# Pooling the keys and values of all later batches on GpSimd instead of VectorE

## Chip, cores and metric

One of the eight cores of a Trainium2 chip runs the whole kernel. The metric is device time in microseconds (us) from launch to end, lower is better. The kernel before was run three times; the profile is of one more execution.

## What is computed

Attention with pooled keys and values over 8 batches of 8 heads, 576 tokens and 64 channels, then a dense feed-forward layer with a piecewise activation, then a layer of eight experts of which each token takes one. The change touches only the pooling of `k` and `v`: the mean over groups of 8 neighbouring tokens, which leaves 72 pooled rows per head.

```python
B, H, S, D = q.shape                      # 8, 8, 576, 64
k_p = k.reshape(B, H, S // 8, 8, D).mean(axis=3)
v_p = v.reshape(B, H, S // 8, 8, D).mean(axis=3)
scores = (1 / sqrt(D)) * q @ k_p^T
x = softmax(scores) @ v_p                 # 4608 tokens x 512
h = x @ w_in; g = activation(h); x = g @ w_out
...                                       # then each token's expert, from the arg max of x @ w_gate
```

## The kernel before

The 4608 tokens are 36 tiles of 128. They go through the dense layer in ten blocks of two to four tiles. A block has 16 steps (`m`), each a group of matmuls with `w_in` (`f1`, lines 624 to 626) and one with `w_out` (`f2`, lines 665 to 669). Every number is split in two parts for precision, so each product takes three matmuls. The order on each engine is the order in which the program text issues the instructions; nothing reorders them.

Between the matmul groups stand *slots*, two per step. A slot runs the next one or two *units* of the attention of the tiles ahead: transposing `q` (`u_qt`, line 346 for tiles from 9 on), scores (`u_sc`, lines 365 to 385, or `u_sc_all`, lines 305 to 316), the softmax's sum and reciprocal (`finish`, lines 394 to 397) and its product, on VectorE for tiles 9 to 33 (line 399) and on GpSimd for the others (line 407), turning the probabilities (`u_turn_p` and `u_place_p`, by way of the DRAM tensor `p_d`, lines 416 and 422), and the product with the pooled values (`u_pv`, line 442 on TensorE, lines 448 and 449 for its eviction). A slot also runs steps of the routing of the block before (`route_steps`); the last of these are scatters by GpSimd into `perm_d` (line 760), which wait for VectorE's line 746 or 747 and for one another.

Pooling: `load_kv` (line 240) is a DMA on the sync engine's queue (SP) that brings one head's keys or values as 72 rows of 8 x 64 numbers into one of three buffers `RAW`. `pool_kv` adds the eight parts. On VectorE it is one `tensor_reduce` (line 246). On GpSimd it is three additions, of 256, 128 and 64 columns, each of the two halves of what is left (lines 249 to 251). Keys go to `KP` (in tile `AT`), which TensorE transposes (`u_kt`, line 290); values go to `VS`, which line 442 reads. Then the same step issues the load of the head three further on into the buffer just freed, so this load waits for the pooling. Batch 0's and batch 1's keys are pooled in other ways (`head_pool`, `pair_step`); the eight values of batch 1 and all sixteen heads of batches 2 to 7 go through `kv_step`. Of these, batches 2 to 7 (96 heads) use VectorE and batch 1 uses GpSimd.

SP is one queue in order. Besides these loads it holds the loads of `q` for the turned tiles (`load_chunk`, line 227, four DMAs of one 32-row part each), the stores of the split `w_out` (line 612, after VectorE's line 261), and lines 416 and 422. A DMA that waits for an engine holds up all that stand behind it. GpSimd (POOL in the profile) is one queue too: scatters, the products of line 407, the low parts of `w_in` (line 261 called with GpSimd, tile `W`) and, now, the poolings.

Of the kernel before, what the change touches and what calls it, by code (L numbers as in the profile page):

```python
# [23 lines left out]
def attention_ffn_routed_experts_kernel(  # L24
# [12 lines left out]
    nc = tc.nc  # L37
# [67 lines left out]
    def at(o, n, p=128):  # L105
        return AT[0:p, o:o + n]
# [10 lines left out]
    RAW = [at(3264 + 512 * i, 512, SP_) for i in range(3)]  # L117
# [120 lines left out]
    def load_kv(b, i, dst):  # L238
        src = k if i < H else v
        nc.sync.dma_start(out=dst, in_=src[b, i % H].rearrange("(p r) d -> p (r d)", r=8))  # L240

    def pool_kv(b, i, raw, eng):
        h = i % H
        dst = (KP if i < H else VS[:, b % 2])[:, h * D:(h + 1) * D]
        if eng is nc.vector:
            eng.tensor_reduce(out=dst, in_=raw.rearrange("p (r d) -> p d r", r=8), axis=AX.X,
                              op=ALU.add)
            return
        eng.tensor_tensor(out=raw[:, 0:256], in0=raw[:, 0:256], in1=raw[:, 256:512], op=ALU.add)
        eng.tensor_tensor(out=raw[:, 0:128], in0=raw[:, 0:128], in1=raw[:, 128:256], op=ALU.add)  # L250
        eng.tensor_tensor(out=dst, in0=raw[:, 0:D], in1=raw[:, D:2 * D], op=ALU.add)
# [209 lines left out]
    def kv_step(b, i):  # L461
        def f():
            n = (b - 1) * 2 * H + i
            pool_kv(b, i, RAW[n % 3], nc.vector if b > 1 else nc.gpsimd)
            if n + 3 < (B - 1) * 2 * H:
                load_kv(1 + (n + 3) // (2 * H), (n + 3) % (2 * H), RAW[n % 3])
        return f
# [111 lines left out]
    n = FIRST  # L579
# [558 lines left out]
    with tc.manual_schedule():  # L1138
# [124 lines left out]
        for g, (j, m) in enumerate(steps):  # L1263
            if m == 0:
# [11 lines left out]
                if j == 1:  # L1276

                    n = 4 * TURN0 // CHUNK
# [204 lines left out]
```

## Time and profile before

| | |
|---|---|
| three runs | 1439.2, 1444.04 and 1445.14 us, median 1444.04 us |
| the profiled execution's own time | 1442.14 us |
| its span, first to last instruction | 1440.4 us |
| TensorE (PE) busy | 1377.1 us, 96% |
| VectorE (DVE) busy | 862.5 us, 60% |
| ScalarE (ACT) busy | 418.3 us, 29% |
| GpSimd (POOL) busy | 183.5 us, 13% |
| mean granted TensorE clock | 0.984 |

The engines run side by side, so no column adds up to the span. Matmuls overlap each other, and a busy PE can hide a slower step; where PE stands still, the list of its waits says on what. "SPq" is the sync engine's queue, "issue" a time for which the profile names no reason.

### The profile page before, as it was taken

What the parts mean: (1) busy time and instruction counts of PE and PEld (TensorE: products, weight loads), DVE (VectorE), ACT (ScalarE), POOL (GpSimd) and SP (SyncE); (2) the same over time, 40 slices, a digit from 0 to 9 for tenths busy, and PEclk for the clock granted to TensorE, in tenths of its full rate; (3) what the DMA queues carried; (4) which work ended last, traced back from release to release, by engine and by line L of the source; (5) the groups of instructions that cost most, each with busy time, mean ns of one, the idle gap of its engine ahead of it and who ended that gap; (6) DMA issues with size and microseconds to landing.
All of it is one profiled execution on the core that took longest, in us unless ns stands there. A gap on an engine that the chain in (4) does not pass through costs nothing. (4 is left out here: it accounts for less than half of the span.)

```text
span 1440.4 us, 21554 instructions
## 1 busy us (share of the span) xinstructions
PE 1377.1 (96%) x7920; PEld 1114.1 (77%) x7920; DVE 862.5 (60%) x1692; ACT 418.3 (29%) x745; POOL 183.5 (13%) x206
## 2 busy tenths in 40 slices
PE   6799999999999999999999999998999999999996
PEld 5666677777877878788788788887878888888785
DVE  4688869768777866986866555454432323332435
ACT  5344323322222322222222233342111111111334
POOL 3152100001001001000010011012221211110211
PEclk9899999999999999999999999999999999999999
DMA  8565556546546445554553345561533223332514
GB/s 236 160 209 176 161 148 201 188 140 181 148 143 179 150 132 166 163 178 126 169 167 108 110 137 164 189 231 55 188 125 107 90 79 99 108 98 82 175 38 146
DMA packets 170827, 210.69 MB, mean 146 GB/s; under 512 B 84199, under 2 KB 114055, under 8 KB 170696
## 3 DMA queue, kind: packets, MB, share of 16 engines
q1 hardware_dynamic: 136120, 103.74, 24.5%
q10 hardware_dynamic: 26784, 83.96, 18.1%
q0 software_dynamic: 7792, 21.35, 4.7%
q8 instruction: 69, 1.13, 0.3%
q14 instruction: 62, 0.51, 0.1%
HBM read 182.93 MB, written 49.66 MB: 161 GB/s over the span
## 5 line engine op out<-in xcount | busy, mean ns | idle before, releaser
L624 PE MATMUL ps<-XT,W 128*128 128x512 f32 (+2 forms) x640 | 246.0, 384 | 4.8 <-DVE FG L653 3.6
L625 PE MATMUL ps<-XT,W 128*128 128x512 f32 (+2 forms) x640 | 237.7, 371 | 1.8 <-DVE XT L449 1.8
L626 PE MATMUL ps<-XT,W 128*128 128x512 f32 (+2 forms) x640 | 237.4, 371 | 1.0 <-POOL W L261 1.0
L632 ACT ACTIVATE FX<-FX,half 128x512 f32<-128x512 f32 (+2 forms) x152 | 104.0, 684 | 397.9 <-DVE FX L631 356.9
L667 PE MATMUL ps<-WO,FG 128*128 128x512 f32 x528 | 211.4, 400 | 0.4 <-DMA WO<-wo_d 0.4
L668 PE MATMUL ps<-WO,FG 128*128 128x512 f32 x528 | 207.1, 392 | 0.0
L669 PE MATMUL ps<-WO,FG 128*128 128x512 f32 x528 | 206.4, 391 | 0.0
L1029 DVE SCALAR_TENSOR_TENSOR FG<-ps,FG 128x512 fp32r<-128x512 f32 (+1 forms) x64 | 43.2, 675 | 181.7 <-ACT FG L1028 171.8
L624 PEld LDWEIGHTS ps<-XT,W 128*128 128x128 f32 x640 | 121.3, 190 | 31.5 <-DVE FG L653 6.0
L631 DVE TENSOR_SCALAR FX<-ps 128x512 f32<-128x512 f32 (+2 forms) x152 | 96.1, 632 | 81.7 <-PE ps L626 81.7
L625 PEld LDWEIGHTS ps<-XT,W 128*128 128x128 f32 x640 | 121.4, 190 | 21.0 <-DVE XT L449 2.9
L626 PEld LDWEIGHTS ps<-XT,W 128*128 128x128 f32 x640 | 121.3, 190 | 20.1 <-POOL W L261 2.0
L642 DVE TENSOR_TENSOR ps<-FX,ps 128x512 f32<-128x512 f32 (+2 forms) x144 | 92.9, 645 | 58.7 <-ACT FX L632 57.7
L760 POOL DMA_INDIRECT perm_d<-idt,POSI x36 | 35.1, 974 | 710.2 <-DVE SM L746 564.4
L643 ACT ACTIVATE FG<-ps 128x512 fp32r<-128x512 f32 (+2 forms) x144 | 81.1, 563 | 141.4 <-DVE ps L642 134.8
L667 PEld LDWEIGHTS ps<-WO,FG 128*128 128x128 f32 x528 | 99.7, 189 | 23.2 <-issue 2.4
L669 PEld LDWEIGHTS ps<-WO,FG 128*128 128x128 f32 x528 | 99.5, 189 | 21.5
L668 PEld LDWEIGHTS ps<-WO,FG 128*128 128x128 f32 x528 | 99.7, 189 | 18.3
L653 DVE TENSOR_TENSOR FG<-ps,FG 128x512 fp32r<-128x512 f32 (+2 forms) x144 | 91.8, 638 | 35.2 <-ACT FG L643 33.7
L1028 ACT ACTIVATE FG<-ps 128x512 fp32r<-128x512 f32 (+1 forms) x64 | 37.4, 585 | 248.8 <-PE ps L1025 225.5
L1023 PE MATMUL ps<-XT,W 128*128 128x512 f32 (+1 forms) x256 | 98.7, 386 | 2.9 <-ACT XT L1007 2.9
L1024 PE MATMUL ps<-XT,W 128*128 128x512 f32 (+1 forms) x256 | 99.0, 387 | 0.3 <-DVE XT L1008 0.2
(239 smaller groups left out, 2177.5 us busy)
## 6 DMA issues: line engine op xcount, KB each, us to landing
WO<-wo_d ACTq DMA_DIRECT2D x128, 512.0 KB
AT<-in_moe_w_dram SPq DMA_DIRECT2D x10, 2048.0 KB
AT<-in_moe_w_dram SPq DMA_DIRECT2D x14, 1024.0 KB
p_d<-AT SPq DMA_DIRECT2D x25, 384.0 KB
AT<-in_v_dram SPq DMA_DIRECT2D x60, 144.0 KB
wo_d<-WO SPq DMA_DIRECT2D x16, 512.0 KB
AT<-in_k_dram SPq DMA_DIRECT2D x56, 144.0 KB
yrow_d<-Y ACTq DMA_DIRECT2D x7, 1032.0 KB
```

The source lines that it names most:

```text
L624: nc.tensor.matmul(o, wi(m, 0, c), xh, start=(c == 0), stop=False)
L625: nc.tensor.matmul(o, wi(m, 0, c), xl, start=False, stop=False)
L626: nc.tensor.matmul(o, wi(m, 1, c), xh, start=False, stop=(c == KD - 1))
L631: nc.vector.tensor_scalar(r, o, -1.0, 1.0, op0=ALU.max, op1=ALU.min)
L632: nc.scalar.activation(out=r, in_=r, func=ACTF.Square, scale=0.5, bias=half)
L642: nc.vector.tensor_tensor(out=o, in0=r, in1=o, op=ALU.max)
L653: nc.vector.tensor_tensor(out=gl, in0=o, in1=r32(gh), op=ALU.subtract)
L667: nc.tensor.matmul(o, gh, WO[:, g % 4, 0], start=(m == 0), stop=False)
L668: nc.tensor.matmul(o, gh, WO[:, g % 4, 1], start=False, stop=False)
L669: nc.tensor.matmul(o, gl, WO[:, g % 4, 0], start=False, stop=(m == KF - 1))
L1023: nc.tensor.matmul(o, e1(0)[:, c, ms], xh, start=(c == 0), stop=False)
L1024: nc.tensor.matmul(o, e1(0)[:, c, ms], xl, start=False, stop=False)
```

## The change

In `kv_step` the engine is now GpSimd for every batch. Nothing else in the program text is different.

```diff
@@ kv_step @@
             n = (b - 1) * 2 * H + i
-            pool_kv(b, i, RAW[n % 3], nc.vector if b > 1 else nc.gpsimd)
+            pool_kv(b, i, RAW[n % 3], nc.gpsimd)
             if n + 3 < (B - 1) * 2 * H:
                 load_kv(1 + (n + 3) // (2 * H), (n + 3) % (2 * H), RAW[n % 3])
```

96 instructions leave VectorE and 288 come to GpSimd; the orders of PE, ACT and SP stay as they were. Three places matter for what follows.

VectorE before, in the second block, around the first transpose of `q` for a turned tile, line 346 (`VS` is the pooled values, `WG<-Y` belongs to the routing, `FX<-ps`, `ps<-FX` and `FG<-ps` to the activation, `WO<-FX` to the split of `w_out`, `XT<-ps` to the eviction of line 449):

```order
L246 TENSOR_REDUCE VS<-AT 72x64
L653 TENSOR_TENSOR FG<-ps_74,FG 128x512
L261 TENSOR_TENSOR WO<-FX,WO 128x512
L631 TENSOR_SCALAR FX<-ps_73 128x512
L346 STREAM_TRANSPOSE AT<-AT 128x512
L246 TENSOR_REDUCE VS<-AT 72x64
L642 TENSOR_TENSOR ps_73<-FX,ps_73 128x512
L690 STREAM_TRANSPOSE WG<-Y 128x512
L449 SCALAR_TENSOR_TENSOR XT<-ps_79,XT 128x4x128
```

The same piece now:

```order
L653 TENSOR_TENSOR FG<-ps_74,FG 128x512
L261 TENSOR_TENSOR WO<-FX,WO 128x512
L631 TENSOR_SCALAR FX<-ps_73 128x512
L346 STREAM_TRANSPOSE AT<-AT 128x512
L642 TENSOR_TENSOR ps_73<-FX,ps_73 128x512
L690 STREAM_TRANSPOSE WG<-Y 128x512
L449 SCALAR_TENSOR_TENSOR XT<-ps_79,XT 128x4x128
```

The poolings are gone, and with them the one that stood between the transpose of `q` and the activation's line 642.

GpSimd before, from the second block on (all scatters of six blocks follow one another):

```order
L1208 MEMSET WG 128x512
L1209 MEMSET WG 128x128
L1215 COPY WG<-ident 32x4x8 x4
L407 TENSOR_TENSOR AT<-AT,ssm_127 128x576
L760 DMA perm_d<-idt,POSI 36864x1 x24
L407 TENSOR_TENSOR AT<-AT,ssm_127 128x576
```

GpSimd now, in the fourth block, where the keys of batch 4 meet the scatters:

```order
L760 DMA perm_d<-idt,POSI 36864x1
L249 TENSOR_TENSOR AT<-AT 72x256
L250 TENSOR_TENSOR AT<-AT 72x128
L251 TENSOR_TENSOR AT<-AT 72x64
L249 TENSOR_TENSOR AT<-AT 72x256
L250 TENSOR_TENSOR AT<-AT 72x128
L251 TENSOR_TENSOR AT<-AT 72x64
L760 DMA perm_d<-idt,POSI 36864x1
L249 TENSOR_TENSOR AT<-AT 72x256
L250 TENSOR_TENSOR AT<-AT 72x128
L251 TENSOR_TENSOR AT<-AT 72x64
L760 DMA perm_d<-idt,POSI 36864x1
```

Poolings now stand behind scatters and in front of them; this is so in three stretches (batches 3, 4 and 5), while the scatters of the later blocks fall between batches.

SP, the same before and now, in the second block: each load of a head (line 240) waits for a pooling, and the loads of `q` stand behind it:

```order
L240 DMA AT<-in_v_dram 72x512
L227 DMA AT<-in_q_dram 32x9x32 x4
L612 DMA wo_d<-WO 128x1024
L240 DMA AT<-in_v_dram 72x512
L227 DMA AT<-in_q_dram 32x9x32 x4
L240 DMA AT<-in_v_dram 72x512
L227 DMA AT<-in_q_dram 32x9x32 x4
L612 DMA wo_d<-WO 128x1024
```

What moved here is only whom the loads of line 240 wait for: GpSimd's line 251 in place of VectorE's line 246.

## Rows read from the trace of the kernel before

**Rows 1.** The page, busy time, share of the span and instructions of each engine.

```profile
PE 1377.1 (96%) x7920; PEld 1114.1 (77%) x7920; DVE 862.5 (60%) x1692; ACT 418.3 (29%) x745; POOL 183.5 (13%) x206
```

**Rows 2.** Busy time by stretch: length, then PE, PEld, DVE, ACT, POOL; clock, DMA share, GB/s.

```profile
137.00:157.00 20.00, 18.09 (x81) 11.51 (x80) 17.81 (x30) 6.58 (x12) 5.52 (x16) 1.00 0.33 110
...
200.00:260.00 60.00, 55.87 (x365) 43.76 (x364) 54.30 (x104) 19.44 (x34) 3.12 (x3) 1.00 0.61 182
...
460.00:720.00 260.00, 259.56 (x1665) 207.97 (x1664) 199.40 (x366) 73.39 (x120) 7.77 (x8) 1.00 0.52 156
```

**Rows 3.** What PE waited for, 137 to 720 us: total us, times, longest.

```profile
PE ps L698 <- issue: 3.5, 1, 3.5
PE ps L442 <- DMA PT<-p_d: 3.4, 4, 1.7
PE ps L624 <- DVE FG L653: 2.3, 3, 1.2
PE ps L624 <- ACT XT L448: 0.9, 1, 0.9
PE ps L442 <- ACT PT L431: 0.6, 1, 0.6
```

**Rows 4.** Key poolings, batches 2 to 7, on DVE (line 246): ns min/median/max, first and last start.

```profile
L246 DVE TENSOR_REDUCE AT<-AT x48: 1000/1058/1083, 137.7 to 690.7; 72x64 f32<-72x512 f32 x48
```

**Rows 5.** Batch 1's value poolings on POOL, 76 to 106 us: busy, mean ns, idle before.

```profile
L249 POOL TENSOR_TENSOR AT<-AT 72x256 f32<-72x256 f32 x8 | 5.9, 732 | 7.9 <-DMA AT<-in_v_dram 7.9
...
L250 POOL TENSOR_TENSOR AT<-AT 72x128 f32<-72x128 f32 x8 | 3.6, 455 | 0.6
L251 POOL TENSOR_TENSOR VS<-AT 72x64 f32<-72x64 f32 x8 | 2.6, 320 | 0.6
```

**Rows 6.** Timeline of DVE, 179 to 190 us: start, duration, instruction, idle before.

```profile
183.56 0.71 DVE L346 STREAM_TRANSPOSE AT<-AT 128x512 f32<-128x512 f32 x1 [4.17 <-DMA AT<-in_q_dram]
184.20 0.99 DVE L246 TENSOR_REDUCE VS<-AT 72x64 f32<-72x512 f32 x1
185.12 0.68 DVE L642 TENSOR_TENSOR ps<-FX,ps 128x512 f32<-128x512 f32 x1
...
187.46 0.69 DVE L449 SCALAR_TENSOR_TENSOR XT<-ps,XT 128x512 fp32r<-128x512 f32 x1 [1.06 <-ACT XT L448]
```

**Rows 7.** Timeline of PE, 182 to 189.5 us.

```profile
188.26 1.51 PE L698 MATMUL ps<-WG 128*32 128x96 f32 x32 [3.48 <-issue]
```

**Rows 8.** Busy time by stretch, the one with the lower clock; columns as in Rows 2.

```profile
186.70:193.50 6.80, 5.24 (x41) 4.23 (x42) 5.25 (x8) 2.83 (x7) 0.00 (x0) 0.50 0.63 151
```

**Rows 9.** Timeline of SP's queue, 174 to 189 us.

```profile
177.76 0.37 SPq L240 DMA_DIRECT2D AT<-in_v_dram  x1
180.05 1.81 SPq L227 DMA_DIRECT2D AT<-in_q_dram  x4
```

**Rows 10.** What SP's queue waited for, 157 to 184 us.

```profile
SPq L240 <- DVE AT L246: 2.0, 3, 0.8
SPq L227 <- DMA FX<-w_d: 1.9, 1, 1.9
SPq L240 <- DVE VS L246: 0.8, 1, 0.8
```

**Rows 11.** What SP's queue waited for, 137 to 720 us.

```profile
SPq L240 <- DVE AT L246: 148.5, 40, 22.1
```

**Rows 12.** Timeline of POOL, 338 to 358 us (scatters of the third block).

```profile
348.50 0.96 POOL L760 DMA_INDIRECT perm_d<-idt,POSI  x1 [5.29 <-DMA perm_d<-idt,POSI]
```

**Rows 13.** Timelines of POOL and of DVE, 60 to 63.5 us.

```profile
60.42 1.30 POOL L261 TENSOR_TENSOR W<-FX,W 128x512 fp32r<-128x512 f32 x1 [20.46 <-ACT W L572]
...
61.12 0.63 DVE L396 TENSOR_SCALAR ssm<-ssm 128x8 f32<-128x8 f32 x1
```

**Rows 14.** Lines 396 and 399, whole span: ns min/median/max, first and last start.

```profile
L396 DVE TENSOR_SCALAR ssm<-ssm x36: 165/172/628, 23.4 to 873.5; 128x8 f32<-128x8 f32 x36
...
L399 DVE TENSOR_TENSOR AT<-AT,ssm x25: 757/757/760, 207.5 to 805.0; 128x576 f32<-128x576 f32 x25
```

## Prediction
> **What bounds the kernel now.** I read the busy times first. TensorE (PE) is busy for 96% of the span, VectorE (DVE) for 60% [rows 1], but a mean says little, so next comes the table by stretch, from the first pooling that moves (137.7 us) to the last (about 717 us). From 460 to 720 us PE is busy for 259.56 of 260 us: whatever DVE does there, PE sets the pace. In two earlier stretches DVE is the fuller engine: 17.81 of 20 us at 137 to 157 us, 54.30 of 60 us at 200 to 260 us, and there PE has holes [rows 2]. What the change can win is therefore the time for which PE stands still between 137 and 720 us, and the list of PE's waits gives it, item by item [rows 3]. DVE's total isn't the measure.
>
> The largest item is the 3.48 us before line 698, at 188.26 us, for which the list has no name [rows 7]. DVE's timeline explains it. At 183.56 us DVE begins the transpose of `q` of line 346 after 4.17 us of waiting for the load of `q`. Everything behind it is late: a pooling of 0.99 us, line 642, ScalarE's evictions, and line 449, which ends at 188.15 us [rows 6]. Line 449 reads the PSUM bank that line 698 needs next, and PE starts 0.11 us later. The standstill has an aftermath: the granted clock is 0.50 from 186.7 to 193.5 us, the lower of the two levels (1.2 in place of 2.4 GHz), and PE is busy for 5.24 us of that [rows 8]. At full clock the same matmuls would have taken half, so 2.6 us go there.
>
> **The change part by part.** *What leaves DVE*: 96 reductions, 48 of keys at 1.058 us and 48 of values at nearly the same [rows 4], about 101 us in all. None of it counts by itself where PE is full; it counts in the waits below.
>
> *What POOL gets*: 96 times three additions of 732, 455 and 320 ns, 1.51 us a head [rows 5], 145 us in 580 us. POOL is at 13% of the span [rows 1], so it has the time. Costed at nothing, under the cover of the load distance: a head's load is issued three poolings ahead, and its pooled rows are used many slots later. If that cover went, SP would stand, and the second rival prices that.
>
> *The end of the first block (137 to 157 us)*: five reductions (5.3 us) leave a DVE that has 2.2 us of slack there [rows 2]. PE's waits on ScalarE in this stretch, 0.9 us on line 448 and 0.6 us on line 431 [rows 3], come from evictions that run late behind DVE. I take both: **1.5 us**. Bounds: 0, if ScalarE is late by itself; 1.9 us, all of PE's idle time there (20 less 18.09) [rows 2].
>
> *The late load of `q`*: the load's last four DMAs are issued at 180.05 to 181.86 us, behind the head load of 177.76 us [rows 9], and DVE starts at 183.56 us. For PE not to stand, line 449 would have to end 3.48 us sooner. One microsecond of it comes for nothing, since the pooling of 0.99 us between the transpose and line 642 [rows 6] is gone. The load must bring the other 2.5 us. On SP, up to there, 2.0 and 0.8 us were waits for poolings on DVE, and 1.9 us, just before these four, a wait for a load `FX<-w_d` [rows 10], which ScalarE issues behind DVE's work. The first two waits go if POOL is in time, which makes 2.8 us at once; the third shrinks, because five reductions (another 5.3 us) no longer stand in DVE's line ahead of it. So the load moves forward by 2.8 to 4.7 us, a little more than the 2.5 us needed. I take the whole standstill, 3.5 us, and with it the 2.6 us of low clock that followed it: **6.1 us**. Bounds: 0, if the `q` rows are limited by their own transfer; 6.1 us.
>
> *Turned probabilities and the second block*: PE waits 3.4 us, in four places, for `PT<-p_d`, and 2.3 us for DVE's line 653 [rows 3]. The second is DVE's lateness, and goes. The first is a load of line 422 that stood in SP behind head loads, and these waited for DVE in total 148.5 us on keys alone [rows 11]. That sum is mostly waiting that cost nothing, but in these four places the transfer behind it was late. POOL, which stands idle most of the time, answers sooner. **5.7 us**; bounds 0 and 5.7 us.
>
> *What the additions do to DVE*: this is the price that could come back. At 60.42 us POOL runs an addition of 1.30 us until 61.72 us; DVE's line 396, of 8 columns, starts at 61.12 us and takes 0.63 us, until 61.75 us [rows 13], where 0.172 us is its median [rows 14]. It ended with POOL's addition. So a small DVE instruction can lose up to 0.45 us to POOL. The Trainium skill, "SBUF — State Buffer", section "Who interferes with whom", has the rule: DVE and GpSimd share a pair of ports, a `tensor_scalar` can take it, a DVE instruction with two SBUF inputs contends too, and the loser waits for the whole instruction. The trace agrees for line 396; no row shows it for line 399, the two-input product of the turned tiles. By that rule each turned tile would have two exposed instructions, and the sum would be the smaller one that follows here.
>
> The price by rows: POOL pools for 145 of 580 us, so an addition is under way a quarter of the time. Line 396 may lose 0 to 0.45 us. Line 399 [rows 14] shows no loss, so 0 is one end; the other is one longest addition, 0.73 us [rows 5]. For a tile that makes a quarter of 1.2 us, 0.3 us, in a chain which reaches PE only where the probabilities are late. If every one of the four late places lost a full 0.3 us, that would be **1.2 us** given back, and I take that; bounds 0 and 4 times 1.2, 4.7 us.
>
> *Sum*: 1.5 + 6.1 + 5.7 − 1.2 = 12.1 us. The profiled execution's own time is 1442.1 us (its span 1440.4 us, and 1.7 us around it); it becomes 1430.0 us. The median of the three runs is 1.9 us above that execution, so the forecast of a median is **1432 us**. After 720 us the program has the same orders and PE is the pace again, so what is won before stays won.
>
> **The rivals.** *The load of `q` is late anyway.* Its four DMAs of many short rows may be bound by their own transfer and by the load `FX<-w_d` [rows 10], not by poolings. Against: 1.0 us is won in the chain regardless, and most of the SP waits named there are for poolings. For: the margin is small, 2.8 against 2.5 us. Then most of the 6.1 us stays, 12.1 − 6.1 = 6 us are won, and the time is 1438 us, within half a per cent.
>
> *The poolings get stuck behind scatters (slower).* POOL is one queue, and in three stretches poolings stand behind scatters of line 760, one of which waited 5.29 us for the scatter before it and then took 0.96 us [rows 12]. A pooling behind such a pair ends up to 5.29 + 0.96 + 1.51 = 7.8 us late; the head load that waits for it stands in SP ahead of line 422, and PE waits for `PT`. The three stretches have some two turned tiles each. If three of the six take the full delay, that is 23 us against 12.1 us won: 1444 + 11 = 1455 us. It decides from the point where the pooling ends after the `p_d` rows have landed. Against it: in the stretch shown, the two poolings whose buffers SP refills before line 422 stand before or right behind the first scatter, not behind the second, and with DVE before them they were late too. It is unlikely.
>
> *Nothing moves.* PE is full, and the holes are filled from behind: each wait that goes uncovers the next one, ScalarE or a load. Then 1444 us. Against it: the holes are few and far apart (five groups in 580 us), and between them PE has no second wait in the list [rows 3].
>
> **How the numbers follow.** The forecast has 0.60, the late load 0.24, nothing 0.09, the slower case 0.07. A measurement of this kernel can tell about 0.5% from no change, 7.2 us. The forecast's 12 us is above that with some room: I count 0.56 of its 0.60 as faster, and 0.05 of the late load's 0.24, where part of the clock's 2.6 us is won. Faster 0.61; within half a per cent 0.32 (0.04 + 0.19 + 0.09); slower 0.07. The range: at its low end all the holes (13.3 us) and nothing given back, and the spread of the runs before, 1439.2 to 1445.14 us, of which I allow 5 us, so 1425 us; at its high end the late load, 1438 us, with all of the price of the additions, 3.5 us more, and so 1442 us. What is left out is the slower case, most of the case in which nothing moves, and the far tails.
>
> **What would show it.** Right: no wait of line 346 for `in_q` near 180 us, no standstill before line 698, and no stretch at clock 0.50 there; PE busy nearly all of 184 to 200 us; no item `PT<-p_d` in PE's list; DVE's busy time about 100 us lower and POOL's 145 us higher; SP's waits for line 251 far below those for line 246. Line 396 with a longer median would show the shared ports, and harmless if PE doesn't wait for it. Wrong: line 346 still waits over 2 us (first rival); PE waits on `PT` longer than before while line 249 stands behind line 760 (second); a new name at the head of PE's list with a sum like the old (third).

## The result and the profile after

The median went from 1444.04 us (7 runs, 1439.2 to 1447.66) to **1429.99 us** (7 runs, 1425.11 to 1437.37). The ratio is 0.9913, with a 95% interval of 0.989 to 0.9936: 0.9% faster, and 2.0 us from the forecast. The profiled execution took 1429.39 us, its span 1427.7 us (before 1442.14 and 1440.4), and the mean granted clock was 0.985 (before 0.984).

The page of the kernel after, first part:

```profile
PE 1374.2 (96%) x7920; PEld 1114.6 (78%) x7920; DVE 781.7 (55%) x1596; ACT 419.1 (29%) x745; POOL 332.1 (23%) x494
```

VectorE lost 80.8 us and GpSimd gained 148.6 us against [rows 1]. VectorE lost less than the 101 us of the poolings; the last section comes back to this. By stretch (columns as in [rows 2]):

```profile
137.00:157.00 20.00, 20.00 (x90) 13.49 (x89) 14.81 (x26) 7.73 (x14) 14.98 (x36) 1.00 0.41 140
184.00:200.00 16.00, 16.00 (x105) 12.94 (x104) 9.67 (x18) 6.14 (x12) 8.35 (x15) 1.00 0.63 189
200.00:260.00 60.00, 58.82 (x352) 47.21 (x351) 43.03 (x87) 21.56 (x37) 27.46 (x48) 1.00 0.69 215
460.00:720.00 260.00, 260.00 (x1682) 208.72 (x1681) 167.46 (x345) 73.70 (x120) 65.06 (x120) 1.00 0.54 155
```

Against [rows 2], PE is now full at 137 to 157 us and misses 1.2 us instead of 4.1 us at 200 to 260 us. The second row covers the stretch where the clock had been 0.50 [rows 8]; it is 1.00 now. At 460 to 720 us VectorE has 32 us less to do, and PE, which was idle for only 0.44 us there, can win next to nothing. What PE waited for, 137 to 720 us; this is the whole list:

```profile
PE ps L442 <- DMA PT<-p_d: 1.2, 1, 1.2
PE ps L698 <- DVE XT L449: 1.1, 1, 1.1
```

The five items of [rows 3] make 10.7 us; the rest of that list is four small ones, 1.1 us together. The wait for `PT<-p_d` that is left isn't one of the old ones made shorter. It is at a line 442 before which PE waited 0.20 us in the kernel before; three longer waits of [rows 3], at 230 to 255 us, stood ahead of it and are gone. On PE's timeline, before and after:

```profile
257.95 1.09 PE L442 MATMUL ps<-PT,VS 72*64 72x128 f32 x16 [0.20 <-DMA PT<-p_d]
```

```profile
245.80 1.09 PE L442 MATMUL ps<-PT,VS 72*64 72x128 f32 x16 [1.18 <-DMA PT<-p_d]
```

The place of the late `q` load, on VectorE's timeline:

```profile
178.46 0.71 DVE L346 STREAM_TRANSPOSE AT<-AT 128x512 f32<-128x512 f32 x1 [3.63 <-DMA AT<-in_q_dram]
179.09 0.67 DVE L642 TENSOR_TENSOR ps<-FX,ps 128x512 f32<-128x512 f32 x1
...
181.43 0.69 DVE L449 SCALAR_TENSOR_TENSOR XT<-ps,XT 128x512 fp32r<-128x512 f32 x1 [1.07 <-ACT XT L448]
```

and the first matmuls after it, on PE's timeline:

```profile
182.18 0.87 PE L698 MATMUL ps<-WG 128*32 128x96 f32 x32 [1.14 <-DVE XT L449]
```

The transpose starts 5.1 us earlier than in [rows 6], line 642 stands right behind it, and PE waits 1.14 us instead of the 3.48 us of [rows 7]. But VectorE still waited 3.63 us for the load. Its DMAs, on SP's timeline, are issued 5.3 us earlier than in [rows 9]:

```profile
174.79 1.84 SPq L227 DMA_DIRECT2D AT<-in_q_dram  x4
```

What SP's queue waited for, 137 to 720 us:

```profile
SPq L416 <- DVE AT L415: 159.2, 18, 19.4
SPq L422 <- DMA p_d<-AT: 47.0, 19, 6.7
...
SPq L240 <- POOL AT L251: 27.1, 17, 5.7
SPq L612 <- DVE WO L261: 22.9, 7, 5.4
...
SPq L240 <- POOL VS L251: 8.5, 9, 1.7
```

The waits of line 240 fell from 148.5 us on keys alone [rows 11] to 35.6 us on keys and values. The queue isn't freer for it: it now stands at line 416 for VectorE's line 415, for 159.2 us. The same list of the kernel before has:

```profile
SPq L416 <- DVE AT L415: 62.2, 13, 18.0
```

To say where the time came from I put the starts of PE's matmuls of both traces in order (both have 7920) and took the difference of the two at the same matmul. This *lead* over the profiled execution of before is worked out from the traces, and used for all runs below. In us, at times of the kernel before:

| kernel | 137 | 160 | 184 | 200 | 262 | 460 | 720 | end |
|---|---|---|---|---|---|---|---|---|
| after | 1.0 | 3.7 | 3.7 | 8.5 | 12.2 | 14.6 | 15.6 | 12.7 |
| after, a second profile (after_again) | −2.3 | 0.5 | 0.5 | 5.1 | 8.6 | 11.1 | 12.1 | 5.0 |

From 137 to 720 us, the stretch of the moved poolings, after wins 14.6 us and its repetition 14.4. Before 137 us nothing was changed, and after 720 us little that matters; there single executions differ by several us either way. So totals need many runs, and leads of the changed stretch need few.

The leads also show that a standstill costs more than the list of waits says. The list counts from the end of the record before it. Where PE runs full, its records overlap: in the same trace, at 152 us, matmuls of 0.39 us start 0.23 us apart. At one stop of the first block, on PE's timeline of the kernel before,

```profile
150.82 0.49 PE L624 MATMUL ps<-XT,W 128*128 128x512 f32 x1 [0.87 <-ACT XT L448]
151.55 0.50 PE L625 MATMUL ps<-XT,W 128*128 128x512 f32 x1 [0.23 <-DVE XT L449]
```

the waits are 1.10 us, and the kernel after, which doesn't stop there, gains 1.62 us of lead over these matmuls and their neighbours.

### The profile page after: what moved, and what is told of

The parts are those of the page before. It is cut to its first block, busy times and chain, and to the rows that moved or that the text cites. A ratio compares the mean times of both kernels' runs of the same rounds, so it can differ in the third digit from the quotient of the medians.

```text
span 1427.7 us, 21825 instructions
## 1 busy us (share of the span) xinstructions
PE 1374.2 (96%) x7920; PEld 1114.6 (78%) x7920; DVE 781.7 (55%) x1596; ACT 419.1 (29%) x745; POOL 332.1 (23%) x494
## 5 line engine op out<-in xcount | busy, mean ns | idle before, releaser
L760 POOL DMA_INDIRECT perm_d<-idt,POSI x36 | 35.6, 988 | 408.6 <-DVE SM L746 343.2
L249 POOL TENSOR_TENSOR AT<-AT 72x256 f32<-72x256 f32 x106 | 78.4, 740 | 172.0 <-DMA AT<-in_v_dram 102.9
L1023 PE MATMUL ps<-XT,W 128*128 128x512 f32 (+1 forms) x256 | 99.0, 387 | 2.6 <-ACT XT L1007 2.6
```

The costliest lines, as they stand in the source:

```text
L1023: nc.tensor.matmul(o, e1(0)[:, c, ms], xh, start=(c == 0), stop=False)
```

## Experiments

The theory: the gain comes place by place, where VectorE was nearly full or a chain through it was late. The rivals: it is VectorE's load as a whole; it is SP's queue, whose head loads GpSimd releases sooner; GpSimd's additions give part of it back, or GpSimd itself is near its limit.

### Only batch 2 moved, and only batches 3 to 7

```diff
-            pool_kv(b, i, RAW[n % 3], nc.gpsimd)
+            pool_kv(b, i, RAW[n % 3], nc.vector if b > 2 else nc.gpsimd)
```

```diff
-            pool_kv(b, i, RAW[n % 3], nc.gpsimd)
+            pool_kv(b, i, RAW[n % 3], nc.vector if b == 2 else nc.gpsimd)
```

> Only batch 2 is pooled on GpSimd, batches 3 to 7 on VectorE as before. Theory 1 (the gain is TensorE's standstills, place by place, and they are independent): the first block's end and the late load of q are repaired, so TensorE's lead over the kernel before is some 7.5 us by 200 us of the span (2.8 us from 137 to 160, 4.7 us from 180 to 200) and stays there; time about 1436 us, standstill before line 698 at about 1.1 us, no low clock near 187 us, waits for PT<-p_d as before. Rival (VectorE's load as a whole counts, 101 us removed for 14 us won): one sixth of it, 2 us, so 1442 us.

> Batch 2 is pooled on VectorE as before, batches 3 to 7 on GpSimd. Theory 1: no lead by 200 us, the standstill of 3.5 us before line 698 and the low clock after it stay; then some 7 us are won (3.7 us at 200 to 262, 2.3 us up to 460, 1 us after); time about 1437 us, and with the run of batch 2 alone the two gains sum to that of the whole change. Rival (VectorE's load as a whole counts): five sixths, 12 us, so 1432 us.

Measured: b2_only 1434.55 us, ratio 0.9949 (0.993 to 0.9968); b3_up 1435.08 us, 0.996 (0.9941 to 0.9979). PE's waits at 137 to 720 us, b2_only:

```profile
PE ps L624 <- DVE FG L653: 2.8, 4, 1.2
PE ps L698 <- DVE XT L449: 2.4, 1, 2.4
PE ps L442 <- DMA PT<-p_d: 1.4, 1, 1.4
```

and b3_up:

```profile
PE ps L442 <- DMA PT<-p_d: 4.4, 3, 2.2
PE ps L698 <- issue: 3.4, 1, 3.4
PE ps L624 <- ACT XT L448: 0.9, 1, 0.9
PE ps L442 <- ACT PT L431: 0.6, 1, 0.6
```

The two gains, 0.51% and 0.40%, add up to the whole, 0.87%. In lead, up to 340 us of the span, they are 7.6 and 3.5 us, nearly after's 11.4. Behind that b2_only loses 2.3 us at its last item (the wait of 1.4 us, at 351.6 us, with the clock at 0.50 for 3.4 us behind it), so that its lead from 137 to 720 us is 6.1 us; b3_up's is 4.8. One batch of six makes about half of the gain, so it isn't VectorE's load as a whole. Batch 2 removes the ScalarE items, all but one of the waits for `PT<-p_d`, and part of the standstill before line 698, of which 2.4 us stay where 1.1 were expected. Batches 3 to 7 remove the waits for line 653 and two of the waits for `PT<-p_d`, but two others grow, so that the item as a whole is larger than in [rows 3]; they won less than the 7 us expected.

### Batches 2 and 3 moved

```diff
-            pool_kv(b, i, RAW[n % 3], nc.gpsimd)
+            pool_kv(b, i, RAW[n % 3], nc.vector if b > 3 else nc.gpsimd)
```

> Batches 2 and 3 are pooled on GpSimd, 4 to 7 on VectorE. Theory (the gain lies where VectorE was nearly full, before some 262 us): 11 to 12 of the 14.6 us of TensorE's lead, time within 3 us of the changed kernel on the same chip, and waits for PT<-p_d and line 653 after 340 us as in the kernel before. Rival (VectorE's load as a whole counts): a third of it, 5 us of lead, 8 us slower than the changed kernel.

Measured: 1434.47 us, ratio 0.9956 (0.9943 to 0.9969), and 7.8 us of lead won to 720 us. That is a miss. Up to 340 us it won 10.2 us (after: 11.4). Then PE waited for turned probabilities, on its timeline:

```profile
347.38 1.09 PE L442 MATMUL ps<-PT,VS 72*64 72x128 f32 x16 [2.34 <-DMA PT<-p_d]
```

and from 349.0 to 352.4 us the clock was 0.50. The lead fell by 3.2 us. So most of the gain is won by 262 us, as the theory has it, but a part of the program without moved poolings can lose it again.

### All poolings moved, VectorE's load kept

The poolings run on GpSimd as in the changed kernel, and VectorE does a reduction of the same shape into a scratch tile that nobody reads.

```diff
             pool_kv(b, i, RAW[n % 3], nc.gpsimd)
+            if b > 1:
+                nc.vector.tensor_reduce(out=DUM, in_=DIN, axis=AX.X, op=ALU.add)
```

> The changed kernel, with a reduction of the old shape (72x512 to 72x64) of data that never change left on VectorE at each of the 96 places; its result is thrown away. VectorE is as full as before, but the head loads in SP's queue wait for GpSimd alone. Theory 1 as the prediction split it: what VectorE's lateness cost comes back (2.8 us at the end of the first block, 1 us in the chain to line 698, 2 to 3 us of line 653), what the queue's release won stays (the waits for PT<-p_d, most of the q load), so about half: 1437 us, 6 to 8 us under before. Rival A (all is VectorE's load): 1444 us, no gain. Rival B (all is the queue's release): 1430 us.

Measured: 1441.96 us, ratio 1.0009 (0.9991 to 1.0027). In the medians nothing is won, and in lead from 137 to 720 us 1.2 us of after's 14.6. PE's longest waits, 137 to 720 us (here the lines stand some numbers lower in the file: 629 is 624, 658 is 653, 703 is 698, 617 is 612):

```profile
PE ps L442 <- DMA PT<-p_d: 3.5, 3, 2.0
PE ps L629 <- DVE FG L658: 3.4, 4, 1.3
PE ps L703 <- DVE XT L449: 2.7, 1, 2.7
```

SP's head loads no longer wait for VectorE, and still the probabilities come as late as before. SP's timeline at one of them shows why:

```profile
220.44 0.93 SPq L240 DMA_DIRECT2D AT<-in_k_dram  x2
225.55 0.35 SPq L617 DMA_DIRECT2D wo_d<-WO  x1
226.00 1.60 SPq L422 DMA_DIRECT2D PT<-p_d  x3
```

with VectorE's timeline (line 469 is the scratch reduction):

```profile
223.26 1.07 DVE L469 TENSOR_REDUCE DUM<-W 72x64 f32<-72x512 f32 x1
...
224.85 0.67 DVE L261 TENSOR_TENSOR WO<-FX,WO 128x512 fp32r<-128x512 f32 x1
```

The head loads pass at 220.44 us, and then the store of the split `w_out` holds the queue until VectorE's line 261 ends, at 225.52 us. Line 422 goes at 226.00 us. In the kernel before the head loads held the queue longer, and line 422 goes no later for it, at 226.22 us:

```profile
221.20 3.70 SPq L240 DMA_DIRECT2D AT<-in_k_dram  x2
...
226.22 1.66 SPq L422 DMA_DIRECT2D PT<-p_d  x3
```

The in-order queue had a second wait right behind the first, on the same engine. One thing is not separated: VectorE was busy for 866.4 us here, 3.9 us more than before, since GpSimd's additions stretch some of its instructions, so a small gain of the queue could be covered by that.

### The order of SP's loads

In the kernel before, `q` loads are issued after a slot's units, one per slot. Here they go ahead of the units, two per slot while more than four are due; no engine's work changes. Done to the kernel before (before_q2) and to the one after (after_q2):

```diff
         def run_units(n):
+            for _ in range(2 if len(qloads) > 4 else 1):
+                if qloads:
+                    qloads.popleft()()
             for _ in range(n):
                 units.popleft()[1]()
-            if qloads:
-                qloads.popleft()()
```

> The kernel before (pooling on VectorE) with only the order of the q loads in SP's queue changed: they stand ahead of the slot's head load, and while more than four are due two are issued in a slot. Theory 1 (the load of q is late because it stands behind head loads): line 346 no longer waits near 180 us, no standstill before line 698, no low clock at 187 us; 4.7 to 6.1 us won there and nothing elsewhere, so about 1439 us. Rival (the q rows are limited by their own transfer, or VectorE's lateness alone makes the standstill): line 346 still waits 2 us or more, and the time is 1444 us.

> The changed kernel with the q loads moved ahead of the slot's head load, two in a slot while more than four are due. Theory (what is left of the standstill before line 698, 1.1 us, is the load of q alone): line 346 has no wait near 178 us, TensorE has no standstill before line 698; 1 to 2 us under the changed kernel, 1428 us, less than the comparison can tell. Rival (the two changes bring the same thing and nothing adds up, or the earlier q loads hold up head loads): the time of the changed kernel or 1 to 3 us more.

Measured: before_q2 1438.63 us, ratio 0.9974 (0.9958 to 0.9991); after_q2 1429.48 us, 0.9926 (0.9905 to 0.9948), the same as after. PE's timeline of before_q2 has line 698 without a wait:

```profile
182.67 0.87 PE L698 MATMUL ps<-WG 128*32 128x96 f32 x32
```

and 6.0 us are won at 184 to 200 us, with the clock at 1.00. So the place of the `q` load in the queue alone makes the difference between the standstill with its low clock and none. From 200 us on it loses 2.5 us again: PE waits 2.33 us for `PT<-p_d` at 350.0 us, where the kernel before waits 0.78 us, and the clock is 0.50 for 3.4 us behind it. after_q2 wins 6.0 us at 184 to 200 us too, where after wins 4.7, and loses 5.5 us at another place, by its PE timeline and its table by stretch (columns as in [rows 2]):

```profile
245.76 1.97 PE L442 MATMUL ps<-PT,VS 72*64 72x128 f32 x16 [2.75 <-DMA PT<-p_d]
```

```profile
245.50:252.40 6.90, 6.64 (x27) 5.38 (x28) 2.58 (x4) 1.71 (x3) 5.29 (x10) 0.51 0.67 237
```

So its lead from 137 to 720 us is 9.7 us, less than after's 14.6. At that place a group of `q` loads stands between the store of the turned probabilities and the loads that bring them back: lines 416, 227 and 422 are issued at 232.82, 234.68 and 237.68 us on SP's timeline. The new order didn't put it there; the changed kernel has it too (234.35, 235.64 and 240.94 us), and so has the kernel before. The next pair of runs takes such loads out of there.

### The same, with no `q` load between line 416 and line 422

```diff
+    held = [False]
+
     def u_turn_p(t):
+        held[0] = True
...
     def u_place_p(t):
+        held[0] = False
...
-                if qloads:
+                if qloads and not held[0]:
```

> The changed kernel with the q loads ahead of the head loads (two a slot while more than four are due) and, between the store of a tile's turned probabilities and their load back, no q load at all. Theory (what is left is two standstills, before line 698 for the load of q and near 244 us for PT<-p_d, whose load stands behind q loads and the transfers they fill): neither is over 0.5 us, TensorE's lead over the kernel before grows by some 16 us from 137 to 720 us, and the time is 2 us under the changed kernel on the same chip. Rival (the load of PT waits for the transfers that ScalarE's queue starts, not for q loads): the wait near 244 us stays at 1.5 us or more.

> The kernel before (pooling on VectorE) with the q loads' order of the last version: ahead of the head loads, two a slot while more than four are due, none between the store and the load back of turned probabilities. Theory (the standstill before line 698 is the queue's order, what is won at the end of the first block and from 200 us on is VectorE's load): 6 us of TensorE's lead from 184 to 200 us as with the first reordering, none from 137 to 160, and under 1.5 us from 200 to 720, where the wait for PT<-p_d near 228 us stays; time 4 to 6 us under before, 1437 us. Rival (all that mattered was the order in SP's queue, the pooling's engine does not count): 12 us or more, 1429 us.

Measured: after_hold **1424.14 us** (6 runs, 1422.79 to 1426.93), ratio 0.9885 (0.9866 to 0.9904), and less than the changed kernel's 1432.08 us in the same series (after_again, below); before_hold 1436.41 us, 0.9957 (0.9937 to 0.9976). after_hold's PE waits at 137 to 720 us, and its stretch at 200 to 260 us:

```profile
PE ps L446 <- DMA PT<-p_d: 1.9, 1, 1.9
```

```profile
200.00:260.00 60.00, 60.00 (x357) 48.41 (x357) 42.50 (x87) 21.71 (x37) 29.86 (x51) 1.00 0.70 221
```

before_hold's longest PE waits, 137 to 720 us (line 446 is 442, 628 is 624, 657 is 653):

```profile
PE ps L446 <- DMA PT<-p_d: 3.0, 3, 1.7
PE ps L628 <- DVE FG L657: 2.8, 4, 1.2
```

The order alone gives 6.0 us at 184 to 200 us, nothing at 137 to 157 us and −0.2 us at 200 to 720 us. VectorE's load gives the rest: with the same order after_hold wins 2.8 us at 137 to 160 us and 5.0 us at 200 to 262 us as well, and the wait at 245.8 us is gone. That is what the theory had. What it did not have is the wait of 1.9 us, at 342.3 us, where after doesn't wait; with the clock at 0.50 from 344.3 to 347.7 us it costs 2.7 us.

Do the two gains add up? In lead from 137 to 720 us they don't: 5.8 us by the order alone, 14.6 by the poolings alone, 13.6 by both, where 16 were expected. The standstill before line 698 is within reach of both, and the new wait takes more. In medians they nearly do: 6.1 us by the order, 9.8 us (after_again) to 14.1 us (after) by the poolings, 17.7 us by both. The difference lies behind 720 us, where the orders of after and after_hold are the same and the profiled executions still part: after_hold won 1.5 us there, after lost 2.9 and after_again 7.1. So why after_hold is the fastest of all isn't shown.

### GpSimd's work doubled, and taken away

pool_twice adds four additions to each moved pooling, into a scratch tile; no_pool has none of the moved poolings on any engine. Its routing comes out another way, so its total, 1400.72 us, is not compared.

```diff
+            if b > 1:
+                double_pool(RAW[n % 3])
             pool_kv(b, i, RAW[n % 3], nc.gpsimd)
```

```diff
-            pool_kv(b, i, RAW[n % 3], nc.gpsimd)
+            if b == 1:
+                pool_kv(b, i, RAW[n % 3], nc.gpsimd)
```

> The changed kernel with GpSimd's pooling work about doubled: before each of the 96 poolings four more additions (three of 72x128, one of 72x64, some 1.7 us) into a scratch tile whose content nobody uses. Theory (GpSimd's additions cost VectorE a few us in lines 396, 261 and 399, 3.6 us in the changed kernel, and none of it reaches TensorE; GpSimd has time to spare): VectorE's lost time doubles to some 7 us, GpSimd is at about 34% of the span, the time stays within 2 us of the changed kernel, 1428 to 1432 us. Rival (the poolings are near the point where they hold up SP's queue behind scatters, or where the shared ports reach TensorE's path): at least 5 us slower than the changed kernel, waits for PT<-p_d in TensorE's list of 5 us or more.

> Nothing pools batches 2 to 7: their loads are issued, and no engine adds; scores and values of these batches use what lies in the buffers. What it leaves out is that pooling, so the routing and with it the end after some 940 us are other work; it is compared by TensorE's lead over the kernel before at 720 us, where the changed kernel has 14.6 us more than at 137 us. Theory (GpSimd's poolings are free): the lead is 14 to 17 us, that is at most 2.4 us more, which are the standstills that were left. Rival (their price, ports or queue, is hidden in the result): 18 us or more.

Measured: pool_twice 1435.29 us, ratio 0.9957 (0.9937 to 0.9977); GpSimd busy 495.0 us, 35%. Half the gain is gone, where the theory had the time unchanged; the lead from 137 to 720 us is 6.6 us in place of 14.6. Its PE waits, 137 to 720 us (lines 708 and 636 are 698 and 626):

```profile
PE ps L442 <- DMA PT<-p_d: 3.4, 1, 3.4
PE ps L708 <- DVE XT L449: 2.7, 1, 2.7
PE ps L636 <- POOL W L261: 1.3, 1, 1.3
```

The first two stand at the two places where after waits, 1.2 and 1.1 us there, and behind each the clock is 0.50 for 3.4 us. The third is a part of `w_in` that GpSimd prepares behind poolings; the kernel before waits 0.2 us for it. Of the two reasons that the expectation names for its rival, the shared ports aren't what grew: VectorE's busy time is 783.5 us, 1.8 us more than after's, and what its lines 261, 396 and 399 lose is 4.5 us as in after (last section). SP's wait for poolings did, from 35.6 us to:

```profile
SPq L240 <- POOL AT L251: 73.7, 27, 9.3
SPq L240 <- POOL VS L251: 64.1, 30, 3.8
```

Against after, 1.5 us of lead are lost at the part of `w_in`, 2.9 at line 698 and 3.8 at line 442. So late answers of GpSimd are the reason that is left; the chain from them to the second and third place was not followed. no_pool won 13.0 us of lead from 137 to 720 us, a little less than the 14 to 17 expected; the clock was 0.50 for 3.4 us at 245 us, and 1.00 throughout in after. It still waits 0.9 and 1.5 us at after's two places. Taking the poolings off GpSimd wins nothing more: as it stands they cost PE nothing that these two profiles can tell, but there is no room for twice the work, though the engine is then idle for 65% of the span.

### The change once more

An unaltered copy, for the spread.

> The changed kernel once more, as the measure for the other two on the same chip and to see how far single executions differ: the same time, 1428 to 1432 us, the same standstills within 1 us each.

Measured: 1432.08 us (6 runs, 1426.25 to 1437.12), ratio 0.993 (0.9907 to 0.9953). The profiled execution was a long one, 1437.12 us, and its lead is the second line of the table above: the gain of the changed stretch is repeated to 0.2 us.

## Why the prediction was right, and where not

- **What counts (right).** PE's standstills between 137 and 720 us were the measure. 12.1 us were forecast; the span became 12.7 us shorter, the median 14.1 us, the lead in the stretch grew by 14.6 us. That 460 to 720 us would give little was right too: 1.0 us of lead. That the time came within 2.0 us of the forecast is in part luck: the four terms were off by +1.3, −1.4, +1.4 and +1.2 us, and after_again, the same kernel, won only 9.8 us in its median.
- **The end of the first block: 1.5 us taken, 2.8 us of lead found** (137 to 160 us), over the bound of 1.9 us. The term was mis-sized, since it went by the two largest waits of the list. PE stops three times there in the kernel before, for 1.9 us by the list, and these stops are worth 0.51, 0.64 and 1.62 us of lead, together the 2.8 us: a stop costs more than its wait. dve_load_kept won 0 there and b2_only all 2.8 us, so the cause, VectorE's load, was right.
- **The late load of `q`: 6.1 us taken, 4.7 us found** (184 to 200 us). The low clock went, as said. The standstill went from 3.48 to 1.14 us and not to nothing. The step that failed is "the whole standstill". The load was issued even earlier than thought, 5.3 us against 2.8 to 4.7, and line 698 starts 6.08 us sooner (182.18 against 188.26 us). But PE arrives there 3.74 us sooner (the lead at 184 us), so only 6.08 − 3.74 = 2.34 us of the standstill were won: the load had to catch up with an earlier PE, not with the old one. The sign "no wait of line 346" was wrong for the same reason: 3.63 us of it were left. The other half of the reason, that the queue's order makes the load late, is shown by before_q2. The rival of a load bound by its own transfer would have left the standstill there, and didn't hold.
- **Turned probabilities and the second block: 5.7 us taken, 7.1 us found** (200 to 720 us), over the bound of 5.7 us, again because a stop costs more than its wait. The waits for line 653 went. Those for `PT<-p_d` fell from 3.4 to 1.2 us, which is not "no item `PT<-p_d`": the old ones went, and another grew from 0.20 to 1.18 us. The step "POOL answers sooner" failed as the reason. In dve_load_kept GpSimd answers as soon, and 3.5 us of waits stay, because SP then stands before the next DMA that needs VectorE, as shown for one of the three. What counts is that VectorE itself is less full.
- **What the additions do to VectorE: 1.2 us taken, none found on PE.** They do stretch VectorE, by 4.5 us in all (last section). The sign named, a longer median of line 396, did not come, 171 ns against 172; single ones lose up to 0.57 us, where the prediction had 0.45. Line 399 loses 0.10 us at most, of the 0.73 it allowed, and line 261, which it had not looked at, up to 0.49. But with VectorE at 43.03 of 60 us no PE wait was traced to them, and no_pool, without them, has no more lead.
- **The rivals.** A pooling stuck behind a scatter was seen, and cost PE nothing. SP's longest wait for GpSimd's line 251, 5.7 us, is in the first block, where no scatter runs. Its longest in a stretch with scatters is 3.8 us, until 347.5 us, for a pooling that starts at 345.83 us, right behind a scatter that had itself waited 1.48 us for the one before; PE has no wait there. pool_twice shows that late poolings were nearer than they looked: the busy share of GpSimd is no guide to it. That each removed wait uncovers the next is what happened on SP's queue and in after_q2, and on PE in the changed kernel once, for the 1.2 us above. "No second wait in the list" went by the five rows shown, which leave out four small waits.

The prediction after 720 us, "what is won before stays won", holds roughly for the medians and not for single executions: after lost 2.9 us of lead there, after_again 7.1, and after_hold won 1.5.

## What to carry to other kernels

Sum the standstills of the engine that sets the pace, place by place, and ask of each which engine the chain behind it is late on: moving work off an engine won most here where that engine was nearly full (17.81 of 20 us, 54.30 of 60 us) or a chain through it ended late, and only 3.3 of 14.6 us in the 458 us behind, where it had room. A wait removed from an in-order queue is worth only the distance to the next wait behind it, so look at the second one before counting the first. The order of loads in a queue can be worth as much as an engine's load: a few lines of order took 6 us off the kernel before, and the fastest kernel here has both, though its traces don't show where the second gain comes from.

## What was not expected of the hardware

**Some instructions of VectorE are held up by GpSimd's additions, and the other way round.** Lines 396, 399 and 261 of the kernel after, at 137 to 720 us (count, then ns min/median/max, first and last start):

```profile
L396 DVE TENSOR_SCALAR ssm<-ssm x24: 165/171/743, 138.9 to 705.0; 128x8 f32<-128x8 f32 x24
...
L399 DVE TENSOR_TENSOR AT<-AT,ssm x22: 757/758/852, 197.6 to 705.4; 128x576 f32<-128x576 f32 x22
...
L261 DVE TENSOR_TENSOR WO<-FX,WO x16: 679/736/1173, 154.2 to 250.4; 128x512 fp32r<-128x512 f32 x16
```

In the kernel before the last group is at 673/680/682 ns. One case, on GpSimd's and on VectorE's timeline:

```profile
153.94 0.74 POOL L249 TENSOR_TENSOR AT<-AT 72x256 f32<-72x256 f32 x1
154.75 0.79 POOL L250 TENSOR_TENSOR AT<-AT 72x128 f32<-72x128 f32 x1
```

```profile
154.15 1.07 DVE L261 TENSOR_TENSOR WO<-FX,WO 128x512 fp32r<-128x512 f32 x1
```

Line 261 starts within line 249's addition and takes 1.07 us; its last 0.54 us lie behind that addition. Line 250, which starts in the meantime, takes 0.79 us where 0.455 is usual [rows 5]. The excess of lines 396, 399 and 261 over their medians in the kernel before is 4.5 us in all, of 580, worked out from the traces. The Trainium skill, "SBUF — State Buffer", section "Who interferes with whom", says that a VectorE instruction with two SBUF inputs contends with a GpSimd instruction that reads SBUF, and a `tensor_scalar` may. The trace agrees for both: 1173 against 680 ns, and 743 against 171 ns. It is also part of why VectorE lost only 80.8 us and not 101. The larger part is that its records overlap, by 0.07 us for the pooling at 184.20 us in [rows 6] (0.99 us long, and the next starts after 0.92): without the 96 poolings, the busy time in the trace of the kernel before is 85.9 us less, where their own times add up to 100.7. With the 4.5 us of the excess that makes 81.4 us, close to the 80.8 found.

**The clock after a standstill.** It was 0.50, the lower of the two levels (1.2 in place of 2.4 GHz), for 6.8 us after the 3.48 us of [rows 7], for 6.9 us after the 2.75 us of after_q2, and for 3.4 us after the 2.34 us of b23_only. It was 0.50 for 3.4 us also after pool_twice's 2.68 us before line 698, after after_hold's 1.89 us and after b2_only's 1.44 us at 351.6 us. After b2_only's 2.38 us and dve_load_kept's 2.68 us before line 698 it stayed at 1.00. So a standstill of 1.4 to 3.5 us may cost another 1.7 to 3.4 us (half of the time at the lower level, an estimate from these times), or not; what decides it was not found.
